# Reordering the prologue of a fused attention and feed-forward kernel: first scores ahead of the last k transposes, kv products between the second scores

## The chip, the cores and the metric

One core of one Trainium2 chip. The metric is the device time of one execution in microseconds (us), and the change is judged against the kernel before in runs on the same chip. Engine names: PE does matmuls, DVE elementwise work, ACT copies and activations, POOL is GpSimd, SP issues the transfers.

## The reference, cut to what matters

Causal linear attention with a decay per head, then a feed-forward part without an activation. B=4, H=8, S=768, D=64; d_model 512, d_ff 1536.

```python
for b in range(nb):                                   # blocks of 64 rows
    intra = einsum('bhic,bhjc->bhij', qb, kb) * Dmask
    intra = einsum('bhij,bhjd->bhid', intra, vb)
    inter = einsum('bhid,bhde->bhie', qb * lam_pow, kv_state)
    out[:, :, sl] = intra + inter
    kv_state = lam_block * kv_state + einsum('bhsd,bhse->bhde', kb_dec, vb)
x = out.transpose(0, 2, 1, 3).reshape(3072, 512)
y = ((x @ w_a) * (x @ w_b)) @ w_out
```

The kernel uses blocks of 128 rows. A **unit** is one such block of one batch with all eight heads: 24 units, six to a batch. For a unit it makes *scores* (k times q, into two PSUM banks called kq), *masks* them on DVE, forms the state st from *kv products*, and sums *intra* (mask times v) and *inter* (state times q) in a bank o; ACT copies o into xT. In profile lines m is a mask, tk, tq and tn are transposes of k, q and of k back, kvd is the eighth bank, of the third and later states, and L320 is line 320 of the kernel. Then the feed-forward part makes products a_ps and b_ps from xT and the weights, DVE multiplies them (ab), and op is the last product.

## The kernel before: the parts concerned

The units run in groups, and each unit's attention work is hung into the feed-forward slots (one a, b pair each) of the group before. Only the first group, units 0 to 3, has no feed-forward part to hide behind: its attention is the **prologue**, and PE's first a_ps waits for it.

```python
GROUPS = (4, 1, 2, 4, 4, 4, 4, 1)
PLAN = { ...                                  # slot, piece, unit; S = scores and masks
    3: [(2, "S", 11), (2, "S", 12)], ... }

def ps_bank(name, shape, dt, hold=False, ffn=False):   # seven PSUM banks, taken in turn
    i = bank["next"]
    while i in bank["held"] or (ffn and i == bank["ffn"]):
        i = (i + 1) % 7
    ...
    bank["next"] = (i + 1) % 7
    return ps_pool.tile(shape, dt, name=name, tag=f"ps{i}")

def prep_k(u):
    early = u < n0 + 3                        # n0 = 4
    make_ks(u, "dve" if early else "pool")    # k times its decay, SBUF to SBUF
    make_qs(u, "pool")
    ...
def prep_v(u):
    make_vb(u, "pool" if u < n0 + 3 else "dve")   # cast of v to bf16, SBUF to SBUF
    pump()                                        # issues further loads

# the prologue, from the transposes on
for w, parts in (("q", 1), ("k", 2)):
    for i in range(2):
        load4(w, i, parts)                    # DVE scales, PE transposes, ACT unpacks
        if w == "q":
            warm(4)                           # four matmuls without use
for u in range(n0):
    make_vb(u, "pool")
scores4(0)                                    # 16 score matmuls, 4 masks
natural_k((0, 1, 2), (0, 1))
warm(2)
natural_k((0, 1, 2), (2, 3))
warm(2)
scores4(1)                                    # the other 16, 4 masks
warm(4)
sts = [ps_bank("kv0", ...), ps_bank("kv1", ...), kv_bank()]   # the last has an eighth bank
for hh in range(2):
    for u, ps in enumerate(sts):
        for w in range(u + 1):
            kv_mms(ps, w, range(2 * hh, 2 * hh + 2), w == 0)
        if hh:
            kv_copy(u, ps, ("act", "act", "dve")[u])          # PSUM to st
intra(0); evac_o(0, *xTs[0])                  # evac_o: o to xT, on ACT if not said otherwise
intra(1); inter(1); evac_o(1, *xTs[1])
intra(2); intra(3)
inter(2); evac_o(2, *xTs[2], eng="dve")
inter(3); evac_o(3, *xTs[3])
natural_k((3,), (0, 1, 2, 3))
# ... then the feed-forward part of group 0
```

Of the kernel before, what the change touches and what calls it, by code (L numbers as in the profile page):

```python
# [17 lines left out]
BF16 = mybir.dt.bfloat16  # L18
# [4 lines left out]
def _bc(ap, dims):  # L23
# [9 lines left out]
PACK = 4  # L33
# [12 lines left out]
        (6, "S", 8), (7, "V", 7), (8, "P", 10), (9, "T", 9), (10, "V", 8), (11, "T", 10),  # L46
        (12, "Q", (7, 8, 9, 10)), (12, "P", 11), (13, "V", 9), (14, "P", 12),
        (14, "O2", (9, 10))],
    3: [(2, "S", 11), (2, "S", 12)],
}  # L50
for _g, _u in ((3, 11), (4, 15), (5, 19)):
    PLAN.setdefault(_g, []).extend(
# [9 lines left out]
def kernel(  # L62
# [11 lines left out]
    nc = tc.nc  # L74
    B, H, S, D = q.shape
    BLK = 128
    NB = S // BLK
# [27 lines left out]
    def ps_bank(name, shape, dt, hold=False, ffn=False):  # L105
# [3 lines that stand above are left out]
        if ffn:  # L109
            bank["ffn"] = i  # L110
        bank["next"] = (i + 1) % 7
        if hold:
            bank["held"].add(i)
        return ps_pool.tile(shape, dt, name=name, tag=f"ps{i}")
# [19 lines left out]
    staged = {}  # L134
# [57 lines left out]
    def warm(n, cols=128):  # L192
        for _ in range(n):
            nc.tensor.matmul(idle_ps[:, :cols], lhsT=idle_sb[:, :128], rhs=idle_sb[:, :cols],  # L194
                             start=True, stop=True, skip_group_check=True)
# [5 lines left out]
    x4 = {}  # L201
    for w, src in (("q", q), ("k", k)):
        x4_r = src[0, :, 0:PACK * BLK, :].rearrange("h (p r) d -> p h (r d)", r=PACK)
        for i in range(2):
            t = wst_pool.tile([128, 1024], F32, name=w + "4", tag="wst")
# [18 lines left out]
    ident = singles.tile([128, 128], BF16, name="ident")  # L224
# [13 lines left out]
    lp_q = singles.tile([128, NT, H, 1], F32, name="lp_q")  # L238
    lp_k = singles.tile([128, NT, H, 1], F32, name="lp_k")
# [24 lines left out]
    def make_vb(u, eng):  # L264
        vb = prep_pool.tile([128, H, D], BF16, name="vb", tag="vb")
        vf = raw.pop((u, "v"))
        if eng == "act":
            nc.scalar.copy(vb, vf)
        else:
            eng_of(eng).tensor_copy(vb, vf)  # L270
        U[u]["vb"] = vb
# [27 lines left out]
    def score_banks():  # L299
        return [ps_bank(f"kq{i}", [128, HP, 128], F32) for i in range(2)]  # L300
# [15 lines left out]
    def mask(kq):  # L316
        ms = []
        for i in range(2):
            m = msk_pool.tile([128, HP, 128], BF16, name=f"m{i}", tag=f"m{i}")
            nc.vector.tensor_mul(m, kq[i], lotri_bc)  # L320
            ms.append(m)
        return ms

    def o_bank(u):
        first = "o" not in U[u]
        if first:
            U[u]["o"] = ps_bank("o_ps", [128, HP, 128], F32)
        return first

    def inter(u):  # L330
        d = U[u]
        if u % NB > 0:
            first = o_bank(u)
            for hp in range(HP):
                nc.tensor.matmul(d["o"][:, hp, :], lhsT=st_bufs[(u - 1) % 4][:, hp, :, :],  # L335
                                 rhs=d["qT"][:, hp, :], start=(first and hp == 0), stop=True,
                                 skip_group_check=True)

    def intra(u):
        d = U[u]  # L340
        first = o_bank(u)
        for hp in range(HP):
            for i in range(2):
                p = slice(64 * i, 64 * i + 64)
                nc.tensor.matmul(d["o"][p, hp, :], lhsT=d["vb"][:, 2 * hp + i, :],  # L345
                                 rhs=d["m"](i, hp), start=(first and hp == 0),
                                 stop=True, skip_group_check=True)

    def evac_o(u, xT, col, eng="act"):
        o_ps = U[u].pop("o")  # L350
        if eng == "act":
            nc.scalar.copy(xT[:, :, col:col + BLK], o_ps)  # L352
        else:
            nc.vector.tensor_copy(xT[:, :, col:col + BLK], o_ps)

    def kv_mms(ps, w, hps, first):
        d = U[w]
        for hp in hps:
            nc.tensor.matmul(ps[:, hp, :, :], lhsT=d["kn"][:, 2 * hp:2 * hp + 2, :],  # L359
                             rhs=d["vb"][:, 2 * hp:2 * hp + 2, :], start=(first and hp == 0),  # L360
                             stop=True, skip_group_check=True)

    def kv_bank():
        kv["ps"] = kvps_pool.tile([128, HP, 2, D], F32, name="kvd", tag="kvd")
        return kv["ps"]
# [8 lines left out]
    def kv_copy(u, ps, eng="dve"):  # L374
        st = st_bufs[u % 4]
        if eng == "act":
            for i in range(2):
                p = slice(64 * i, 64 * i + 64)
                nc.scalar.copy(st[p, :, i, :], ps[p, :, i, :])  # L379
        else:  # L380
            nc.vector.tensor_mul(st[:].rearrange("p hp i d -> p hp (i d)"),  # L381
                                 ps[:].rearrange("p hp i d -> p hp (i d)"), bdiag_bc)
# [110 lines left out]
    xs4 = {"q": scr[0][:, 0:4, :], "k": scr[1][:, 0:4, :]}  # L493
    xT4 = {"q": scr[0][:, 4:8, :], "k": scr[1][:, 4:8, :]}
    kn4 = scr[1][:, 8:12, :].rearrange("p u (h d) -> p u h d", d=D)

    def load4(w, i, parts):
        dst = xs4[w].rearrange("p r (h d) -> p r h d", d=D)
        tab = lp_q if w == "q" else lp_k
        for j in range(2):  # L500
            if j == 0 or parts == 2:
                tps = ps_bank("t" + w, [128, 2, PACK, 128], BF16)
            hs = slice(4 * i + 2 * j, 4 * i + 2 * j + 2)
            nc.vector.tensor_mul(
                dst[:, :, hs, :].rearrange("p r h d -> p h r d"),
                x4[w, i][:, :, 2 * j:2 * j + 2].rearrange("p r h d -> p h r d"),
                tab[:, NB:, hs, :].rearrange("p r h o -> p h r o").to_broadcast([128, 2, PACK, D]))
            for r in range(PACK):
                nc.tensor.transpose(tps[:, j, r, :],
                                    xs4[w][:, r, hs.start * D:hs.stop * D], ident)  # L510
            if parts == 2:
                unpack(i, tps, slice(j, j + 1), w)
                if i == 0 or j == 0:
                    warm(3)
        staged.pop((w + "4", i))
        if parts == 1:
            unpack(i, tps, slice(0, 2), w)

    def unpack(i, tps, js, w):
        nc.scalar.copy(xT4[w][:, 2 * i + js.start:2 * i + js.stop, :]  # L520
                       .rearrange("c hp (p r) -> c hp p r", r=PACK),
                       tps[:, js].rearrange("c j r p -> c j p r"))

    def natural_k(us, hps):
        nu, nh = len(us), len(hps)
        tps = ps_bank("tn", [128, nu, nh, 128], BF16)
        for a, u in enumerate(us):
            for b, hp in enumerate(hps):
                nc.tensor.transpose(tps[:, a, b, :], xT4["k"][:, hp, u * BLK:(u + 1) * BLK], ident)
        nc.scalar.copy(kn4[:, us[0]:us[0] + nu, 2 * hps[0]:2 * (hps[0] + nh), :]  # L530
                       .rearrange("p u h d -> p u (h d)"),
                       tps[:].rearrange("p u j x -> p u (j x)"))

    ms4 = {}

    def scores4(i):
        kqs = []
        for up in range(PACK // 2):
            kq = score_banks()
            for uu in range(2):  # L540
                cols = slice((2 * up + uu) * BLK, (2 * up + uu + 1) * BLK)
                for j in range(2):
                    for par in range(2):
                        p = slice(64 * par, 64 * par + 64)
                        nc.tensor.matmul(kq[par][:, 2 * uu + j, :],
                                         lhsT=xT4["k"][p, 2 * i + j, cols],
                                         rhs=xT4["q"][p, 2 * i + j, cols],
                                         start=True, stop=True, skip_group_check=True)
            kqs.append(kq)
        for up, kq in enumerate(kqs):  # L550
            ms4[i, up] = mask(kq)

    for u in range(n0):
        U[u] = dict(kn=kn4[:, u], qT=xT4["q"][:, :, u * BLK:(u + 1) * BLK],
                    m=lambda i, hp, u=u: ms4[hp // 2, u // 2][i][:, 2 * (u % 2) + hp % 2, :])
    for w, parts in (("q", 1), ("k", 2)):
        for i in range(2):
            load4(w, i, parts)
            if w == "q":
                warm(4)  # L560
    for u in range(n0):
        make_vb(u, "pool")
    scores4(0)
    natural_k((0, 1, 2), (0, 1))
    warm(2)
    natural_k((0, 1, 2), (2, 3))
    warm(2)
    scores4(1)
    warm(4)
    sts = [ps_bank("kv0", [128, HP, 2, D], F32), ps_bank("kv1", [128, HP, 2, D], F32), kv_bank()]  # L570
    for hh in range(2):
        for u, ps in enumerate(sts):
            for w in range(u + 1):
                kv_mms(ps, w, range(2 * hh, 2 * hh + 2), w == 0)
            if hh:
                kv_copy(u, ps, ("act", "act", "dve")[u])
    intra(0)
    evac_o(0, *xTs[0])
    intra(1)
    inter(1)  # L580
    evac_o(1, *xTs[1])
    intra(2)
# [73 lines left out]
```

## Time and profile before

| | before |
|---|---|
| time, median of the first runs | 237.72 us (237.71 to 237.79) |
| span of the profiled execution | 235.4 us |
| busy PE, DVE, ACT, POOL | 225.1, 115.7, 92.9, 49.4 us |
| first a_ps, from the chain of waits | 19.35 us |
| PE's waits after 20 us | 0.63 at 57.46 (on DVE), 0.30 at 101.60 (on a DMA transpose) |

The lines of the prologue itself stand in the prediction.

### The profile page before, as it was taken

Reading aid. Unit: us, or ns where it says so; the run is one execution under the profiler, and the core shown is the slowest. Engines: PE = TensorE matmul, PEld = TensorE weight load, DVE = VectorE, ACT = ScalarE, POOL = GpSimd, SP = SyncE. Lnnn points to the kernel's source line nnn. Section 1 sums busy time; section 2 is a strip of 40 time slices with the busy share of each in tenths; the row PEclk is TensorE's granted clock in tenths of the full one; section 3 lists DMA queues with packets and bytes.
Section 4 is the critical chain, followed back from the end, with each engine's and each line's share of the span. In section 5 each row is a group of like instructions: output and inputs, shape, how many; then the busy total and the mean of one; then the engine's idle time right before and its main releaser. Section 6 shows DMA issues by size and latency. Waiting matters only on the chain.

```text
span 235.4 us, 4530 instructions
## 1 busy us (share of the span) xinstructions
PE 225.1 (96%) x1755; PEld 126.2 (54%) x1778; DVE 115.7 (49%) x205; ACT 92.9 (39%) x174; POOL 49.4 (21%) x63
## 2 busy tenths in 40 slices
PE   7699999998999999999999999999999999999994
PEld 2475444448698654444544454544454544444493
DVE  0886566637469637565135665135564215332050
ACT  3567654065565542341142241242341242431161
POOL 6041000245346453103306403003300000000000
PEclk9999999999999999999999999999999999999999
DMA  4999999999999999998919959523120220000311
GB/s 153 301 287 349 349 367 284 292 213 286 204 234 204 223 183 257 183 187 152 242 72 220 177 70 239 140 77 79 26 47 0 89 89 5 0 0 3 133 46 49
DMA packets 94278, 38.32 MB, mean 163 GB/s; under 512 B 81200, under 2 KB 89776, under 8 KB 94256
## 3 DMA queue, kind: packets, MB, share of 16 engines
q1 hardware_dynamic: 94112, 38.02, 71.0%
q8 instruction: 14, 0.23, 0.4%
q14 instruction: 8, 0.07, 0.1%
q10 hardware_dynamic: 144, 0.00, 0.0%
HBM read 28.32 MB, written 6.29 MB: 147 GB/s over the span
## 4 chain that ended last, share of the span: by engine, by line
PE 85%; DMA 6%; DVE 2%; ACT 2%; issue 2%; SPq 1%; DVEq 0%; ACTq 0%
PE op L434 26%; PE a_ps L413 25%; PE b_ps L413 24%; DMA k<-in_k_dram 3%; DMA qkT<-qk 3%; PE o_ps L345 2%; PE kq L308 2%; DVE m L320 2%; PE kvd L359 2%; PE o_ps L335 1%; PE tps L294 1%; ACT xT L352 1%; ACT o_sb L429 1%; SPq L206 1%; ACT st L379 1%
## 5 line engine op out<-in xcount | busy, mean ns | idle before, releaser
L425 DVE TENSOR_TENSOR ab<-a_sb,b_ps 128x512 bf16<-128x512 bf16 (+2 forms) x96 | 52.7, 553 | 82.3 <-PE b_ps L413 61.2
L413 PE MATMUL a_ps<-xT,wa_sb 128*128 128x512 bf16 (+2 forms) x378 | 76.7, 325 | 1.6 <-DVE ab L425 0.6
L413 PE MATMUL b_ps<-xT,wb_sb 128*128 128x512 bf16 (+2 forms) x379 | 76.7, 325 | 0.2
L420 ACT CAST a_sb<-a_ps 128x512 bf16<-128x512 f32 (+2 forms) x96 | 45.6, 481 | 65.6 <-PE a_ps L413 63.4
L434 PE MATMUL op<-wo_sb,ab 128*128 128x512 bf16 (+2 forms) x300 | 64.2, 362 | 0.9 <-issue 0.5
L413 PEld LDWEIGHTS <-wb_sb 128*128 128x128 bf16 x384 | 34.5, 98 | 28.7
L413 PEld LDWEIGHTS <-wa_sb 128*128 128x128 bf16 x384 | 33.5, 98 | 28.2 <-issue 1.6
L434 PEld LDWEIGHTS <-ab 128*128 128x128 bf16 x312 | 28.6, 98 | 30.2
L320 DVE TENSOR_TENSOR m<-kq,lotri 128x512 bf16<-128x512 f32 x48 | 29.9, 683 | 20.5 <-PE kq L308 19.6
L256 POOL TENSOR_TENSOR qk<-kf,lp_k 128x512 bf16<-128x512 f32 x17 | 17.9, 1053 | 76.9 <-issue 31.4
L429 ACT COPY o_sb<-op 128x512 f32<-128x512 f32 (+2 forms) x26 | 14.2, 554 | 37.2 <-PE op L434 36.7
L261 POOL TENSOR_TENSOR qk<-qf,lp_q 128x512 bf16<-128x512 f32 x20 | 23.1, 1154 | 23.8 <-DMA qf<-in_q_dram 23.8
L352 ACT CAST xT<-o_ps 128x512 bf16<-128x512 f32 x23 | 12.4, 590 | 16.9 <-PE o_ps L345 16.9
L381 DVE TENSOR_TENSOR st<-kvd,bdiag 128x512 bf16<-128x512 f32 x18 | 12.3, 684 | 3.8 <-PE kvd L359 3.8
L296 ACT COPY qkT<-tps 128x1024 bf16<-128x1024 bf16 x7 | 7.1, 1012 | 10.9 <-PE tps L294 10.9
L270 DVE CAST vb<-vf 128x512 bf16<-128x512 f32 x17 | 8.4, 496 | 0.0
L194 PE MATMUL idle<-idle_sb 128*128 128x128 bf16 (+1 forms) x38 | 7.2, 322 | 1.3 <-DVE idle_sb L189 1.3
L345 PE MATMUL o_ps<-m,vb 128*64 128x128 bf16 x192 | 7.8, 222 | 0.0
L270 POOL CAST vb<-vf 128x512 bf16<-128x512 f32 x7 | 4.3, 613 | 15.5 <-DMA vf<-in_v_dram 13.8
L308 PE MATMUL kq<-qkT 64*128 64x128 bf16 x160 | 6.7, 218 | 0.3 <-DMA qkT<-qk 0.3
L335 PEld LDWEIGHTS <-st 128*128 128x128 bf16 x80 | 5.4, 98 | 2.8
L345 PEld LDWEIGHTS <-vb 128*64 128x64 bf16 x192 | 5.7, 109 | 1.4
(52 smaller groups left out, 85.3 us busy)
## 6 DMA issues: line engine op xcount, KB each, us to landing
vf<-in_v_dram SPq DMA_DIRECT2D x24, 256.0 KB, 5.2
out_dram<-o_sb SPq DMA_DIRECT2D x23, 256.0 KB, 2.3
qf<-in_q_dram SPq DMA_DIRECT2D x20, 256.0 KB, 4.5
kf<-in_k_dram SPq DMA_DIRECT2D x20, 256.0 KB, 5.1
wst<-in_moe_w_a_dram SPq DMA_DIRECT2D x6, 512.0 KB, 8.7
wst<-in_moe_w_b_dram SPq DMA_DIRECT2D x6, 512.0 KB, 8.8
wst<-in_moe_w_out_dram SPq DMA_DIRECT2D x6, 512.0 KB, 8.5
q<-in_q_dram SPq DMA_DIRECT2D x2, 512.0 KB, 5.4
```

What stands on the lines that cost most here:

```text
L256: eng_of(eng).tensor_mul(qk[:, 1], raw.pop((u, "k")), lp_k[:, u % NB].to_broadcast([128, H, D]))
L261: eng_of(eng).tensor_mul(U[u]["qk"][:, 0], raw.pop((u, "q")), lp_q[:, u % NB].to_broadcast([128, H, D]))
L270: eng_of(eng).tensor_copy(vb, vf)
L320: nc.vector.tensor_mul(m, kq[i], lotri_bc)
L345: nc.tensor.matmul(d["o"][p, hp, :], lhsT=d["vb"][:, 2 * hp + i, :], rhs=d["m"](i, hp), start=(first and hp == 0), stop=True, skip_group_c ...
L352: nc.scalar.copy(xT[:, :, col:col + BLK], o_ps)
L381: nc.vector.tensor_mul(st[:].rearrange("p hp i d -> p hp (i d)"), ps[:].rearrange("p hp i d -> p hp (i d)"), bdiag_bc)
L413: nc.tensor.matmul(ps[:, :gt], lhsT=w_sb[:, s, f * 128:(f + 1) * 128], rhs=xT[:, s, :gt], start=(s == 0), stop=(s == KS - 1))
L420: nc.scalar.copy(a_sb[:, :gt], ps[:, :gt])
L425: nc.vector.tensor_mul(ab[:, f, :gt], a_sb[:, :gt], ps[:, :gt])
L429: nc.scalar.copy(o_sb[:, lo:hi], op[:, lo:hi])
L434: nc.tensor.matmul(op[:, lo:hi], lhsT=ab[:, f, t * 128:(t + 1) * 128], rhs=wo_sb[:, f, lo:hi], start=(f == 0), stop=(f == FC - 1))
```

## The change

The intent: the scores of the first half of the heads need no more than the first two pairs of k, so they can be issued ahead of the last k transposes, and DVE's masks start sooner. PE's wait before the second scores is then filled with kv products of units 0 and 1 in place of warm matmuls. The scores of units 11 and 12 move by one slot. The core of the diff (load4 is split into scale4 and part_k, and kv_part(u, hps) is the old inner loop over w, the kv products of one state for these head pairs; the definitions are left out):

```diff
-    3: [(2, "S", 11), (2, "S", 12)],
+    3: [(3, "S", 11), (3, "S", 12)],
...
-    for w, parts in (("q", 1), ("k", 2)):
-        for i in range(2):
-            load4(w, i, parts)
-            if w == "q":
-                warm(4)
+    ...                                # q as before
+    for i, j in ((0, 0), (0, 1), (1, 0)):
+        scale4("k", i, j)
+        part_k(i, j)
+        warm(3)
+    scale4("k", 1, 1)
     for u in range(n0):
         make_vb(u, "pool")
-    scores4(0)
+    scores4(0, (0, 1))
+    part_k(1, 1)
     natural_k((0, 1, 2), (0, 1))
     warm(2)
     natural_k((0, 1, 2), (2, 3))
     warm(2)
-    scores4(1)
-    warm(4)
     sts = [ps_bank("kv0", ...), ps_bank("kv1", ...), kv_bank()]
-    for hh in range(2): ...            # both halves of kv0, kv1, kv2, copies after the second
+    scores4(1, (0,))                   # 8 of the 16 second scores
+    kv_part(0, (0, 1))
+    kv_part(1, (0, 1))
+    scores4(1, (1,))
+    kv_part(2, (0, 1))
+    for u in range(2):
+        kv_part(u, (2, 3))
+        kv_copy(u, sts[u], "act")
     intra(0)
     evac_o(0, *xTs[0])
     intra(1)
+    kv_part(2, (2, 3))
+    kv_copy(2, sts[2], "dve")
     inter(1)
```

Because the banks are taken in turn, a change of order deals them anew. As the built order has it:

| tile | banks before | banks after | what the user waits for after the change |
|---|---|---|---|
| first scores | 6, 0, 1, 2 | 5, 6, 0, 1 | nothing that comes late |
| kv0, kv1 | 2, 3 | 5, 6 | masks 1 and 2 (before, kv0: mask 4) |
| second scores | 5, 6, 0, 1 | 0, 1, then 2, 3 | masks 3 and 4 (before: mask 1, then 2 and 3) |
| o of units 0 to 3 | 4, 5, 6, 0 | 4, 5, 6, 0 | units 1 and 2: ACT's copies of kv0 and kv1 (before: masks 5 and 6) |

More of the change, by code (lines that the diff above doesn't have):

```diff
@@ L495, with scale4, transpose4, packed_bank @@
     kn4 = scr[1][:, 8:12, :].rearrange("p u (h d) -> p u h d", d=D)
-    def load4(w, i, parts):
-        dst = xs4[w].rearrange("p r (h d) -> p r h d", d=D)
-        tab = lp_q if w == "q" else lp_k
-        for j in range(2):
-            if j == 0 or parts == 2:
-                tps = ps_bank("t" + w, [128, 2, PACK, 128], BF16)
-            hs = slice(4 * i + 2 * j, 4 * i + 2 * j + 2)
-            nc.vector.tensor_mul(
-                dst[:, :, hs, :].rearrange("p r h d -> p h r d"),
-                x4[w, i][:, :, 2 * j:2 * j + 2].rearrange("p r h d -> p h r d"),
-                tab[:, NB:, hs, :].rearrange("p r h o -> p h r o").to_broadcast([128, 2, PACK, D]))
-            for r in range(PACK):
-                nc.tensor.transpose(tps[:, j, r, :],
-                                    xs4[w][:, r, hs.start * D:hs.stop * D], ident)
-            if parts == 2:
-                unpack(i, tps, slice(j, j + 1), w)
-                if i == 0 or j == 0:
-                    warm(3)
-        staged.pop((w + "4", i))
-        if parts == 1:
-            unpack(i, tps, slice(0, 2), w)
+    def scale4(w, i, j):
+        hs = slice(4 * i + 2 * j, 4 * i + 2 * j + 2)
+        nc.vector.tensor_mul(
+            xs4[w].rearrange("p r (h d) -> p h r d", d=D)[:, hs],
+            x4[w, i][:, :, 2 * j:2 * j + 2].rearrange("p r h d -> p h r d"),
+            (lp_q if w == "q" else lp_k)[:, NB:, hs, :].rearrange("p r h o -> p h r o")
+            .to_broadcast([128, 2, PACK, D]))
+        if j == 1:
+            staged.pop((w + "4", i))
+    def transpose4(w, i, j, tps):
+        h = 4 * i + 2 * j
+        for r in range(PACK):
+            nc.tensor.transpose(tps[:, j, r, :], xs4[w][:, r, h * D:(h + 2) * D], ident)
+    def packed_bank(w):
+        return ps_bank("t" + w, [128, 2, PACK, 128], BF16)
+    def part_k(i, j):
+        tps = packed_bank("k")
+        transpose4("k", i, j, tps)
+        unpack(i, tps, slice(j, j + 1), "k")
     def unpack(i, tps, js, w):
@@ L534, with scores4 @@
     ms4 = {}
-    def scores4(i):
+    def scores4(i, ups):
         kqs = []
-        for up in range(PACK // 2):
+        for up in ups:
             kq = score_banks()
@@ L549, in scores4 @@
             kqs.append(kq)
-        for up, kq in enumerate(kqs):
+        for up, kq in zip(ups, kqs):
             ms4[i, up] = mask(kq)
@@ L555 @@
                     m=lambda i, hp, u=u: ms4[hp // 2, u // 2][i][:, 2 * (u % 2) + hp % 2, :])
-    for w, parts in (("q", 1), ("k", 2)):
-        for i in range(2):
-            load4(w, i, parts)
-            if w == "q":
-                warm(4)
+    for i in range(2):
+        tps = packed_bank("q")
+        for j in range(2):
+            scale4("q", i, j)
+            transpose4("q", i, j, tps)
+        unpack(i, tps, slice(0, 2), "q")
+        warm(4)
+    for i, j in ((0, 0), (0, 1), (1, 0)):
[3 more added lines that the diff above has]
+    scale4("k", 1, 1)
     for u in range(n0):
         make_vb(u, "pool")
-    scores4(0)
+    scores4(0, (0, 1))
+    part_k(1, 1)
     natural_k((0, 1, 2), (0, 1))
@@ L567, with kv_part @@
     warm(2)
-    scores4(1)
-    warm(4)
     sts = [ps_bank("kv0", [128, HP, 2, D], F32), ps_bank("kv1", [128, HP, 2, D], F32), kv_bank()]
-    for hh in range(2):
-        for u, ps in enumerate(sts):
-            for w in range(u + 1):
-                kv_mms(ps, w, range(2 * hh, 2 * hh + 2), w == 0)
-            if hh:
-                kv_copy(u, ps, ("act", "act", "dve")[u])
+    def kv_part(u, hps):
+        for w in range(u + 1):
+            kv_mms(sts[u], w, hps, w == 0)
+    scores4(1, (0,))
[6 more added lines that the diff above has]
+        kv_copy(u, sts[u], "act")
     intra(0)
```

## The prediction

> **What bounds the kernel now.** I read the page first. PE is busy in 225.1 of 235.4 us and the chain that ended last is PE for 85%: almost all of it is the feed-forward products (a_ps, b_ps, op). In the row of 40 slices PE stands at 9 from the second or third slice to the last but one, and the granted clock at 9 (full) everywhere. So a change outside the feed-forward part can only pay through the moment at which its first matmul starts, and through the few waits of PE afterwards. Next I read the chain of waits from 0 to 24 us, because that is where this change acts; these are its lines from the last k transposes to that first matmul (start, duration, what):
>
> ```profile
> 11.69 0.40 PE tk L509 x4
> 12.09 0.38 PE kq L545 x8
> 12.46 0.01 DVEq L320
> 12.47 0.04 issue
> 12.52 1.90 DVE m L320 x3
> 14.42 0.04 issue
> 14.46 0.38 PE kq L545 x7
> 14.84 0.33 PE idle L194 x4
> 15.17 0.48 PE kv L359 x6
> ...
> 17.34 0.37 ACT st L379
> 17.71 0.02 issue
> 17.73 1.57 ACT xT L352 x3
> 19.30 0.04 issue
> 19.35 0.38 PE a_ps L413
> ```
>
> The reader is to see three hand-overs: masks on DVE free a bank for the second scores; kv products feed the four st copies on ACT; ACT then makes three xT copies back to back, and the last releases the first a_ps at **19.35**. The timelines of DVE, ACT and PE from 5 to 24 us show how full those stretches are:
>
> ```profile
> 12.52 4.88 DVE L320 TENSOR_TENSOR m<-kq,lotri 128x512 bf16<-128x512 f32 x8 [0.89 <-PE kq L545]
> 17.31 0.68 DVE L381 TENSOR_TENSOR st<-kvd,bdiag 128x512 bf16<-128x512 f32 x1
> ...
> 16.19 1.52 ACT L379 CAST st<-kv 64x256 bf16<-64x256 f32 x4 [1.57 <-PE kv L359]
> 17.73 1.56 ACT L352 CAST xT<-o_ps 128x512 bf16<-128x512 f32 x3
> ```
>
> DVE runs eight masks without a gap, one every 0.60 us; ACT is without a gap from 16.19 to 19.29. Beyond that, PE's waits after 20 us are 0.63 at 57.46 (on DVE), 0.30 at 101.60 (unit 14's DMA transpose) and crumbs.
>
> **What the Trainium skill says.** "TensorE: Matmul & The Clock Gate", section "The mechanism", says that matmuls start and end strictly in program order. So a matmul that waits for its bank holds back everything behind it; the trace agrees, the warm matmuls and kv products stand still behind the scores that wait 0.39 us for a mask at 14.46. The same page, "What's actually happening", puts the fall of the clock at about 3.4 us of idleness; the longest idle time here is under 1.3 us and the clock stays full, and I count on that below. "PSUM — Partial Sum Buffer", section "PSUM bank collisions raise a hardware error", asks that PSUM be guarded by bank rather than by address; the kernel does so, each tile has a bank of seven taken in turn, and its next user waits for the last reader. That decides this case.
>
> **The change part by part.** I followed the turns of the banks and the waits in the built instruction order.
>
> *First scores earlier.* In the old order they start at 12.02, behind the last k transposes, which wait for DVE until 11.69. Now they follow the third k transposes (11.08, four at 0.056 = 0.23) and three warm matmuls (0.17), plus the 0.1 us that the old trace takes between transposes and scores: 11.59, a gain of **0.43**. DVE's last scaling ends at 11.63, so it does not hold the masks: they start at 12.09, the fourth starts at 13.89 and ends at 14.58 (0.68 long).
>
> *Second scores later.* Before, their banks were those of the last k transposes, then of masks 1, 2 and 3, so nine of sixteen ran at 13.57 and the rest at 14.46. Now the two banks of the kv products are taken first (from masks 1 and 2), and the very first scores need the banks of masks 3 and 4. So eight scores start at 14.62. The seven behind the wait take 0.31 as before: 14.93. Mask 5 starts at 15.17 instead of 14.92, DVE has a gap of about 0.5, and mask 8 ends at 17.65 instead of 17.40. The gain of 0.43 is spent.
>
> *kv in between, four warm matmuls gone.* From 14.93: six kv products (6 x 0.056 = 0.33), eight scores (0.31), six kvd products (0.33), the two that finish kv0 (0.11), and 0.2 for three changes of kind: issue ends at 16.21, the last start is one slot of 0.056 earlier, a product lasts 0.22, so kv0 is complete at 16.37 and the first st copy starts at **16.4**, against 16.19. Before, kv0 itself waited for mask 4 (its semaphore at 15.0), with 14 products and no scores behind the wait.
>
> *New waits.* The outputs o of units 1 and 2 now get the banks of kv0 and kv1, so intra(1) waits until ACT has copied st0 and intra(2) until it has copied st1. Before they had the banks of masks 5 and 6 and did not wait: PE ran intra 0 and 1 at 16.58 as one block of 16. Now intra(0) runs at 16.45, ACT's two st0 copies take 0.75 and end at 17.16, and intra(1) starts at 17.2. Behind it, in order: eight intra 0.28, a change 0.06, six kvd 0.33, inter(1) 0.22, a change 0.1, sixteen intra 0.57, eight inter 0.45, two changes 0.15 = 2.16, so the last inter(3) issues by 19.3 and lands near 19.5. st2 is on the same road (kvd ends 18.07, DVE to 18.8) but does not come last. ACT has done xT of units 0 and 1 by 19.0, so the last xT waits for PE: 19.5 + 0.59 = 20.1, first a_ps at **20.15**. That is **+0.8**.
>
> *Scores of units 11 and 12 one slot later.* One slot is an a, b pair, 1.73 us. At the old place they start at 91.38 without a wait, and the masks follow DVE's product at once; one slot on it is the same picture, with four masks (2.48) before the next product and the same rotation of banks. Their masks are used ten microseconds later, at 101.9. I count **0**; it gives the transpose of unit 12 slack that the old trace does not need.
>
> **How much of 0.8 arrives.** PE is full afterwards, so a late start moves the end one for one, except where PE waits for a transfer that does not move with it. The wait at 101.60 can swallow up to 0.3: DMA share is 9 tenths until about 112 us and its queue there is issued without gaps. The wait at 57.46 follows DVE work tied to PE's own slots and stays. So +0.5 to +0.8. I shade it down a little, to **+0.5**, because a turn of banks that I misread would remove the largest term: 237.72 + 0.5 = 238.2.
>
> **Rivals.** *The reorder pays as meant:* the masks start 0.43 earlier, the kv products fill PE's wait, and everything moves up, 237.3. For it: DVE's eight masks are a gapless 4.88 us that end at 17.40, and starting them earlier is the right aim. Against it: mask 5 cannot start before scores that now wait for mask 4. It needs ACT's st copies to start by 15.9. *Absorbed altogether:* if the DMA sets the pace to 112 us, a late start is caught up at the waits for loads and transposes, 237.7. For it: DMA at 9 tenths for half the run. Against: PE shows only 0.30 of wait on DMA after 20 us, and a wait can't give back more than it has. *A wait at the moved scores:* if masks one slot later hold DVE's products and PE finds no free bank, up to 0.6 more, 238.8. For it: the like stall at 57.46, after scores. Against: no stall followed the same block at slot 2.
>
> **Range and chances.** The three cases and the main one lie between 237.3 and 238.9, all within 0.5%. Repeats spread 0.08 us. A change of 2% is 4.75 us, more than the whole idle time that could be won (10.3 us of PE idle, half of it before the first q arrives) and six times the loss that I find. Range 237.4 to 238.8; faster 0.01, same 0.98, slower 0.01.
>
> **What would show each step.** Right: first scores at 11.6 and masks from 12.1; a PE wait on a mask until about 14.6; a gap inside DVE's masks; PE waiting on ACT's st copies at intra(1), near 17.2; first a_ps near 20.1; the wait for unit 14's transpose gone or smaller. Wrong: a_ps before 19.35 would mean that ACT got kv0 much earlier than 16.4, so that I have the banks or the issue rates wrong. A first a_ps near 20.1 with an unchanged total would mean the absorption; a clock below full early on, or new idle time of PE near 94, would mean causes that I left out.

## More of the kernel before

How to read it: each digit of this cut from the page of the kernel before is the busy share of one of 40 slices, in tenths.

```profile
PE   7699999998999999999999999999999999999994
DVE  0886566637469637565135665135564215332050
POOL 6041000245346453103306403003300000000000
DMA  4999999999999999998919959523120220000311
```

The 8 of PE's row is the slice from 53.0 to 58.9 us; POOL and DVE both work there, and that turns out to matter.

## The result, and the profile after

The changed kernel took **238.24 us** (median of four runs: 238.01, 237.62, 238.69, 238.46) against 237.72 of the kernel before (four runs, 237.71 to 237.79). The ratio is 1.0019 [0.9995, 1.0044], so the two are the same within 2%. Ratios here and below are the mean time of one kernel's fast runs over that of the other's of the same rounds, so not quite the ratio of the medians quoted; a ratio is turned into us by 237.5. All outputs are right.

The prologue of the changed kernel, from its chain of waits (start, duration, what):

```profile
12.12 2.50 DVE m L320 x4
...
14.66 0.38 PE kq L546 x7
15.04 0.44 PE kv L359 x6
15.48 0.33 PE kq L546 x8
15.81 0.44 PE kvd L359 x6
16.25 0.13 PE kv L359 x2
...
16.46 0.18 ACT st L379
...
17.26 0.41 PE o_ps L345 x8
...
19.49 0.59 ACT xT L352
20.09 0.04 issue
20.13 1.89 PE a_ps L413 x8
```

The masks start at 12.12 instead of 12.52, and yet the second scores start at 14.66 instead of 14.46: they now wait for the fourth mask. Scores and three groups of kv products follow without a gap, so ACT gets kv0 at 16.46 instead of 16.19. The first a_ps is at 20.13 instead of 19.35, **0.78 later**.

The timeline of DVE in the changed kernel (start, duration, count at the end, in brackets the idle time before it and what ended it):

```profile
12.12 2.49 DVE L320 TENSOR_TENSOR m<-kq,lotri 128x512 bf16<-128x512 f32 x4 [0.46 <-PE kq L546]
15.04 2.48 DVE L320 TENSOR_TENSOR m<-kq,lotri 128x512 bf16<-128x512 f32 x4 [0.43 <-PE kq L546]
```

The eight masks that ran as one block of 4.88 us are now two blocks with 0.43 us of idle time between them. What the early start gained, this gap spends: DVE releases the last masks at 17.52 instead of 17.40.

Now the rest of the run. PE's shift (time after less time before, same instructions) is +0.78 at the first a_ps, +0.42 at 57.46, +0.71 at 74.82, +0.22 at 101.93, and a constant +0.39 from 116 us to PE's last instruction. (The +0.22 is of one moment: the next a_ps, at 102.50 before, is already 0.40 late.) So half of the lateness seen at 20 us was gone in the end, and not in a straight line. Two places matter. The first, from the timelines of all engines, kernel before:

```profile
55.62 1.04 POOL L256 TENSOR_TENSOR qk<-kf,lp_k 128x512 bf16<-128x512 f32 x1 [1.40 <-DMA kf<-in_k_dram]
56.17 1.04 DVE L256 TENSOR_TENSOR qk<-kf,lp_k 128x512 bf16<-128x512 f32 x1
56.62 1.49 POOL L261 TENSOR_TENSOR qk<-qf,lp_q 128x512 bf16<-128x512 f32 x1
...
57.46 0.38 PE L413 MATMUL a_ps<-xT,wa_sb 128*128 128x128 bf16 x4 [0.63 <-DVE ab L425]
```

and the same of the changed kernel:

```profile
56.03 1.04 POOL L256 TENSOR_TENSOR qk<-kf,lp_k 128x512 bf16<-128x512 f32 x1 [2.26 <-DMA kf<-in_k_dram]
56.95 0.68 DVE L256 TENSOR_TENSOR qk<-kf,lp_k 128x512 bf16<-128x512 f32 x1
57.03 1.50 POOL L261 TENSOR_TENSOR qk<-qf,lp_q 128x512 bf16<-128x512 f32 x1
...
57.88 0.33 PE L413 MATMUL a_ps<-xT,wa_sb 128*128 128x128 bf16 x3 [0.27 <-DVE ab L425]
```

The DVE line is the k scaling of unit 6, with both inputs in SBUF. It took 1.04 us before and 0.68 after, and PE's wait behind it fell from 0.63 to 0.27, exactly as much. So 0.36 of the old wait is time that DVE stood still; the other 0.27 is there too when the scaling is not held, and no wait is left where the scaling is taken off DVE (below). In the kernel before, the scaling starts while POOL's k scaling of the next unit runs, and it ends at 57.21, 0.59 after POOL's hand-over at 56.62; POOL's next instruction then lasts 1.49 instead of 1.04. In the changed kernel DVE arrives at 56.95, just as POOL finishes, and gets in ahead of POOL's next one. The Trainium skill has this: "SBUF — State Buffer", section "Who interferes with whom", says that DVE and GpSimd share one pair of ports as an exclusive lock, held for a whole instruction while the loser stands still, and that a DVE instruction with two SBUF inputs contends with a GpSimd instruction that reads SBUF. The traces agree: in each of these meetings one of the two instructions is long.

The second place is the wait on unit 14's DMA transpose, from the timelines of PE, before and after:

```profile
101.60 0.40 PE L308 MATMUL kq<-qkT 64*128 64x128 bf16 x8 [0.30 <-DMA qkT<-qk]
```

```profile
101.60 0.62 PE L308 MATMUL kq<-qkT 64*128 64x128 bf16 x16
```

The 0.30 us of waiting is gone: the eight scores of the unit run in one block with the eight of the unit ahead, and PE's shift falls from 0.70 at 100.58 to 0.40 at 102.50.

Working the other way, DVE's casts of v, which also copy from SBUF to SBUF, became longer. From the page, before and after (busy us, mean ns):

```profile
L270 DVE CAST vb<-vf 128x512 bf16<-128x512 f32 x17 | 8.4, 496 | 0.0
```

```profile
L270 DVE CAST vb<-vf 128x512 bf16<-128x512 f32 x17 | 9.5, 559 | 0.0
```

A cast takes 0.42 undisturbed and up to 1.18 us in these two profiles when it meets POOL. One of them, at 71.86 in the changed kernel, took 0.90 instead of 0.42 (at 71.43) and stands ahead of the masks on DVE; that is where the shift of PE went up again to +0.71.

The profiled span grew by 0.9 where PE's end moved by 0.39. The other 0.5 lies in the last stores, which ended later after PE in that one execution; the next profile of the same kernel had the tail of the kernel before.

### The profile page after: what moved, and what is told of

It reads as the page before. It is cut to its first block, busy times and chain, and to the rows that moved or that the text cites. A ratio compares the mean times of both kernels' runs of the same rounds, so it can differ in the third digit from the quotient of the medians.

```text
span 236.3 us, 4544 instructions
## 1 busy us (share of the span) xinstructions
PE 227.3 (96%) x1774; PEld 126.3 (53%) x1774; DVE 116.6 (49%) x205; ACT 92.8 (39%) x174; POOL 49.1 (21%) x63
## 4 chain that ended last, share of the span: by engine, by line
PE 90%; DMA 3%; DVE 2%; ACT 2%; issue 1%; SPq 1%; DVEq 0%; ACTq 0%
PE a_ps L413 27%; PE b_ps L413 26%; PE op L434 26%; DMA k<-in_k_dram 3%; PE o_ps L345 2%; PE kq L308 2%; PE kvd L359 2%; PE o_ps L335 2%; PE tps L294 1%; DVE m L320 1%; ACT o_sb L429 1%; SPq L206 1%; ACT xT L352 0%; PE kq L546 0%; DVE scratch L499 0%
## 5 line engine op out<-in xcount | busy, mean ns | idle before, releaser
L434 PE MATMUL op<-wo_sb,ab 128*128 128x512 bf16 (+2 forms) x312 | 65.6, 363 | 0.0
L352 ACT CAST xT<-o_ps 128x512 bf16<-128x512 f32 x23 | 12.5, 590 | 16.9 <-PE o_ps L345 16.4
L270 DVE CAST vb<-vf 128x512 bf16<-128x512 f32 x17 | 9.5, 559 | 0.0
```

The source lines that it names most:

```text
L270: eng_of(eng).tensor_copy(vb, vf)
L352: nc.scalar.copy(xT[:, :, col:col + BLK], o_ps)
L434: nc.tensor.matmul(op[:, lo:hi], lhsT=ab[:, f, t * 128:(t + 1) * 128], rhs=wo_sb[:, f, lo:hi], start=(f == 0), stop=(f == FC - 1))
```

## The experiments

Theory after the first look: **the late start is real and explains the whole loss; behind it the DVE and POOL lock and one DMA wait give part of it back or add to it, according to how the two engines happen to meet.** Rivals: (R1) the slot move costs or gains something; (R2) the loss is not the start but something else that the new prologue brings, say transfers; (R3) the scatter of the changed kernel is noise of the chip and has nothing to do with the lock. Five rounds were run of each kernel, on three chips, with runs of the kernel before in each; first a_ps is from the one profiled execution of each.

### The changed kernel again

No edit.

> The changed kernel once more, for its interval. Theory (a late start of the feed-forward part, 0.78 us at the first a_ps, partly given back at later waits): 0.3 to 0.8 us over the kernel before, first a_ps at 20.1. Rival (the 0.5 us between the two medians is only the scatter of the end of the run): within 0.15 us of the kernel before.

238.27 us (237.81 to 239.18, six runs) against 237.28 of the kernel before; ratio 1.0048 [1.0029, 1.0067], some 1.1 us. First a_ps at 20.11. So it is slower by an interval that excludes zero, though still the same by the bound of 2%, and by more than the 0.3 to 0.8 us that were expected. Its runs scatter by 1.4 us: over both sets the ten runs lie from 237.62 to 239.18. The scaling of unit 6 took 0.78 this time. The kernel before in these rounds: 236.44 to 237.80 over eleven runs, so its own spread is not the 0.08 us of the first three runs either.

### The prologue alone

In the changed kernel:

```diff
-    3: [(3, "S", 11), (3, "S", 12)],
+    3: [(2, "S", 11), (2, "S", 12)],
```

> The new prologue with the scores of units 11 and 12 at their old slot 2. Theory (the slot costs nothing, all comes from the prologue): first a_ps at 20.1 and a total within 0.3 us of the changed kernel. Rival (the later slot itself costs or pays): a total at least 0.4 us away from the changed kernel, and new PE idle time near 91 us or near 102 us.

237.91 us (237.51 to 239.22), ratio 1.0036 [1.0016, 1.0057], not to be told apart from the changed kernel. First a_ps at 20.07. Its profiled execution was the slowest of the six, and its timeline shows why a run can be slow:

```profile
55.87 1.04 POOL L256 TENSOR_TENSOR qk<-kf,lp_k 128x512 bf16<-128x512 f32 x1 [2.08 <-DMA kf<-in_k_dram]
56.87 1.04 POOL L261 TENSOR_TENSOR qk<-qf,lp_q 128x512 bf16<-128x512 f32 x1
56.89 1.56 DVE L256 TENSOR_TENSOR qk<-kf,lp_k 128x512 bf16<-128x512 f32 x1
```

DVE came at 56.89, when POOL's second instruction had started at 56.87. It stood still until POOL was done and ended at 58.45, and PE waited 1.15 us behind it. In the changed kernel DVE came at 56.95 and POOL's second instruction at 57.03, with DVE first. A few hundredths of a us decide between a wait of 0.27 and one of 1.15.

### The slot move alone

In the kernel before:

```diff
-    3: [(2, "S", 11), (2, "S", 12)],
+    3: [(3, "S", 11), (3, "S", 12)],
```

> The kernel before, with only the scores of units 11 and 12 one slot later. Theory (the slot is worth nothing): first a_ps at 19.35 as before, scores at 93.1, total within 0.25 us of the kernel before. Rival (the slot carries part of the 0.5 to 1 us): a total 0.4 us or more above the kernel before, with a longer PE wait near 101.6.

237.67 us (237.47 to 237.84) against 237.48; ratio 1.0009 [0.9997, 1.0020]. First a_ps at 19.30. The move costs at most half a us and probably nothing. In its profile the scaling of unit 6 came early enough to be ahead of POOL (0.68), so PE was ahead by 0.4 at 57 (and the moved scores started at 92.70, not 93.1); then it waited 1.15 us at 102.04 for unit 14's transpose, 0.85 more than the kernel before. That longer wait is the sign that the rival named, but the trace does not lead it back to the moved scores: POOL's k scaling after a load was late before they ran (88.03 against 87.52 in the kernel before), the transpose was issued at 95.75 instead of 95.32, and PE came 0.4 earlier. So R1 is out for the size of the loss; one profile can't exclude a small share.

### The start delayed in the kernel before

```diff
     scores4(1)
-    warm(4)
+    warm(18)
```

> The kernel before with 14 more warm matmuls ahead of the kv products, 14 x 0.056 = 0.78 us of pure delay and no other change of order or bank. Theory (only the late start counts): kv products at 15.9, first a_ps at 20.1, PE waits near 57 and 101 smaller than before, and a total 0.3 to 0.6 us over the kernel before, like the changed kernel. Rival (the new order costs by itself later on): first a_ps at 20.1, yet a total within 0.2 us of the kernel before.

238.20 us (237.62 to 238.47), ratio 1.0038 [1.0022, 1.0054]; first a_ps at 20.09. The old prologue with nothing but a start as late as in the changed kernel costs as much as the changed kernel does. So R2 is not needed: the late start is enough. The loss, 0.9 us, is more than the 0.3 to 0.6 expected, and one of the expected signs failed: the wait near 57 grew. The scaling of unit 6 started at 56.91 behind a POOL instruction that had begun at 56.59, and took 1.26; PE waited 0.85 there and nothing at 102.

### The two kv banks withheld from o

In the changed kernel, so that o of units 1 and 2 get other banks and do not wait for ACT's copies:

```diff
     scores4(1, (1,))
     kv_part(2, (0, 1))
+    bank["held"].update((5, 6))
```

> The changed kernel, but the outputs o of units 1 and 2 may not take the banks of kv0 and kv1. Theory (intra(1) waits for the two st0 copies because of the shared bank, and that is on the path): the wait before intra(1) goes, intra(1) at 16.8, st2 on DVE near 17.7, first a_ps at 19.65, that is 0.45 to 0.5 earlier than 20.13 and 0.3 later than before; total 0.1 to 0.4 us over the kernel before. Rival (only the late st copies on ACT set the start): first a_ps stays near 20.1.

First a_ps at 19.61, half a us earlier, and the 16 intra matmuls are one block again. The timeline of ACT in this kernel:

```profile
16.46 1.51 ACT L379 CAST st<-kv 64x256 bf16<-64x256 f32 x4 [1.86 <-PE kv L359]
18.00 1.56 ACT L352 CAST xT<-o_ps 128x512 bf16<-128x512 f32 x3
```

The st copies start when they did in the changed kernel, and now the three xT copies follow without a gap, where the changed kernel's last one waited for PE. So of the 0.78, some 0.5 is the new wait for the kv banks, and the remaining 0.27 is the later st copy. The time was 237.82 (237.66 to 238.12), ratio 1.0025 [1.0012, 1.0038]: of the half us some 0.3 to 0.5 arrived (1.0025 against 1.0036 and 1.0048, with intervals that overlap), and the distance to the kernel before, 0.6, is above the 0.1 to 0.4 expected. The scaling of unit 6 took 1.23 in the profile, and PE waited 0.82.

### A prologue that does what was meant

In the changed kernel the banks are dealt by hand and the kv products of units 0 and 1 go entirely ahead of the last eight scores, with the st copies:

```diff
+    bank["next"] = 5
+    scores4(1, (0,))
+    bank["next"] = 2
     sts = [ps_bank("kv0", ...), ps_bank("kv1", ...), kv_bank()]
...
-    scores4(1, (0,))
     kv_part(0, (0, 1))
     kv_part(1, (0, 1))
-    scores4(1, (1,))
-    kv_part(2, (0, 1))
     for u in range(2):
         kv_part(u, (2, 3))
         kv_copy(u, sts[u], "act")
+    bank["next"] = 0
+    scores4(1, (1,))
+    bank["next"] = 4
+    kv_part(2, (0, 1))
     intra(0)
```

> The changed kernel with the banks dealt anew: the first four second scores take the banks of masks 1 and 2, kv0 and kv1 those of early k transposes, and kv0 and kv1 are finished before the rest of the second scores. Theory: no wait for mask 4 ahead of kv, first st copy on ACT near 15.0, masks on DVE without a gap and ended at 17.0, first a_ps at 18.7 to 18.8, 0.6 before the kernel before; total 0.1 to 0.8 us below it, by how the scalings near 57 fall. Rival (the start is bound by DVE or by the k load, whatever the banks): first a_ps at 19.3 or later.

The timelines of DVE and ACT in this kernel:

```profile
12.11 4.87 DVE L320 TENSOR_TENSOR m<-kq,lotri 128x512 bf16<-128x512 f32 x8 [0.45 <-PE kq L546]
```

```profile
15.03 1.51 ACT L379 CAST st<-kv 64x256 bf16<-64x256 f32 x4 [0.44 <-PE kv L359]
...
18.31 0.59 ACT L352 CAST xT<-o_ps 128x512 bf16<-128x512 f32 x1 [0.53 <-PE o_ps L335]
```

The masks are one block again and start early, the st copies begin at 15.03, and the first a_ps is at 18.95: 1.2 us ahead of the changed kernel and 0.4 ahead of the kernel before (0.6 was expected). So the aim of the change was sound: masks that start early can bring the first a_ps forward. This variant changes the banks and also the order, so it does not show that the banks alone defeated the change; what they cost through o is the 0.5 of the run before. The time, 236.86 (235.97 to 237.74), ratio 0.9976 [0.9957, 0.9996], scatters by 1.8 us.

### The same kernels with the meetings of DVE and POOL removed

Two edits take the two kinds of SBUF to SBUF instruction that met POOL off DVE: the k scaling of unit 6 goes to POOL, the casts of v from unit 7 on go to ACT. They were applied to the kernel before, the changed kernel, and the two variants above:

```diff
-        early = u < n0 + 3
+        early = u < n0 + 2
...
-        make_vb(u, "pool" if u < n0 + 3 else "dve")
+        make_vb(u, "pool" if u < n0 + 3 else "act")
```

> The kernel before, with the k scaling of unit 6 moved from DVE to POOL and the v casts of units 7 and later moved from DVE to ACT, so that no DVE instruction of the stretch from 55 to 80 us can be held up by a POOL instruction. Theory (the PE wait at 57.46 and the later ones come from DVE operations held until POOL's current one ends): the wait of 0.63 near 57 goes, total 0.5 to 0.9 us below the kernel before. Rival (DMA sets the pace there): the wait moves to a load, total unchanged.

> The changed kernel with the same two moves. Theory: first a_ps at 20.1, no wait near 57, so the late start of 0.78 us arrives nearly whole: 0.5 to 0.8 us above before_nolock, and single runs within 0.5 us of each other where the changed kernel spreads over 1.3 us. Rival (the scatter and the give-back come from DMA): spread as wide as that of the changed kernel, difference to before_nolock under 0.4 us.

> after_nolock, with the banks of kv0 and kv1 kept from the outputs o. Theory (the shared bank costs 0.5 us of the 0.78 at the start, and without the scalings and casts on DVE it arrives): first a_ps at 19.6 to 19.7, total 0.3 to 0.55 us below after_nolock, within 0.35 us of before_nolock. Rival (the bank wait was hidden by something else in the end): total within 0.15 us of after_nolock.

> early_st (first a_ps at 18.95) with the same two moves off DVE. Theory: no wait near 57, spread under 0.5 us where early_st spread over 1.8, total 0.3 to 0.7 us below before_nolock, so 235.6 to 236.0. Rival (DMA, that is the transpose of unit 14 near 101, caps what an early start can win): a PE wait there of 0.5 us or more and a total within 0.2 us of before_nolock.

| kernel, without the meetings | first a_ps | time, us | ratio to before | in us |
|---|---|---|---|---|
| early st | 18.99 | 235.62 (235.51 to 235.72) | 0.9923 [0.9911, 0.9934] | -1.8 |
| before | 19.64 | 236.27 (236.01 to 236.42) | 0.9949 [0.9937, 0.9961] | -1.2 |
| changed, kv banks withheld | 19.66 | 236.38 (236.04 to 236.52) | 0.9950 [0.9937, 0.9963] | -1.2 |
| changed | 20.20 | 236.81 (236.74 to 236.97) | 0.9974 [0.9962, 0.9986] | -0.6 |

The time follows the first a_ps one for one: 1.21 us from the first row to the last in both columns (20.20 less 18.99; 0.0051 times 237.5). The spread from the lowest to the highest run fell from 1.4 to 0.2 us in the changed kernel, from 1.8 to 0.2 in the early st variant, from 0.7 to 0.4 in the kernel before (same rounds), and stayed at 0.5 in the one with withheld banks. (The 1.4 and the 0.2 of the changed kernel are of two chips; on the chip of the 0.2, the early st variant spread by its 1.8 and the kernel before by 0.7.) One caution: the 19.64 of the kernel before is of an execution whose first q load came late (19.30 and 19.35 in two others with the same prologue), and that kernel kept a wait of 0.24 us on unit 14's transpose. A start of about 19.35 plus that wait gives the same place.

R3 falls: the large scatter goes when these instructions leave DVE. The kernel before gained 1.2 us, more than the 0.5 to 0.9 expected. The edits also take the scaling and 17 casts off DVE altogether, so how much of the 1.2 us is the lock and how much is a DVE with less to do is not separated by these runs; at the wait near 57 of the kernel before it was 0.36 and 0.27.

The early st variant with these edits beats both kernels, by 1.85 us against 237.47 of the kernel before in its rounds.

### Only the k scaling of unit 6 moved

```diff
-        early = u < n0 + 3
+        early = u < n0 + 2
```

in the changed kernel, casts left on DVE.

> The changed kernel with only the k scaling of unit 6 moved to POOL; the v casts stay on DVE. Theory (the scaling that meets POOL's pair near 57 us makes most of the scatter, the v casts near 72 and 76 the rest): no PE wait near 57, spread about half that of the changed kernel, total about 237.2 to 237.8. Rival (the v casts make it all): spread over 1 us still, total near 238.2.

237.48 us (237.08 to 237.84), ratio 1.0001 [0.9987, 1.0014]; first a_ps at 20.12, and no wait near 57. The standard deviation of its runs is 0.32 us, against 0.54 of the changed kernel's six and 0.09 with the casts moved too. So this one instruction on DVE is part of the scatter and of the loss: without it the late start no longer shows in the time against the kernel before, which still has it. How the casts share the rest with the lighter load of DVE stays open, as said.

### One thing seen, not settled

Unit 14's transpose took 6.1 to 6.3 us from issue to landing in all four kernels with the old prologue, and 4.6 to 5.0 in all nine with a new one. The DMA's busy tenths from 98 to 101 us and the queue of instruction fetches in that stretch, kernel before:

```profile
DMA  9999999999999000000001000010000079999999
q8 instruction: 1, 0.02, 2.6%
```

and the DMA's row of the changed kernel, where no fetch falls into the stretch:

```profile
DMA  9999999999999999999900079999998689999999
```

In the four old ones one fetch of 0.02 MB falls between 98 and 99 us, within the transpose, and for over a us the queues move nearly nothing; in the nine others that fetch comes at 101 us or later. This is thirteen profiles agreeing, and no experiment: why the fetch moved, and whether it holds up the transpose, is open.

## Why the prediction was right, and where its steps were not

- **First scores and masks.** Predicted 11.59 and 12.09, found 11.62 and 12.12. Right.
- **Second scores wait for mask 4.** Predicted 14.62, found 14.66, with one score ahead of it at 14.06. The gap inside the masks was to be 0.5 and was 0.43. Right.
- **First st copy** 16.4, found 16.46; **intra(1) waits for ACT** at 17.2, found 17.26 with 0.33 us of waiting; **last xT waits for PE** at 19.5, found 19.49; **first a_ps** 20.15, found 20.13. Right, and the withheld banks show the term of the kv banks alone: 0.5 of the 0.78.
- **Slot move, 0.** The run of it alone gives 1.0009 with an interval that holds 1. Right.
- **The wait at 101.60 can swallow up to 0.3.** It did vanish. In the delayed kernel before, with the old transposes, it vanished for the reason given: PE came later. In the changed kernel there was a second reason, a transpose that landed sooner (5.0 us after its issue instead of 6.2), which the prediction had not seen. Nor did the transfer stay where it was, as the prediction had assumed: it was issued at 95.89 instead of 95.32.
- **"The wait at 57.46 follows DVE work tied to PE's own slots and stays."** This step failed. The wait was 0.27 to 0.37 in the two profiles of the changed kernel and 1.15 in the one with the prologue alone. What varies in it is DVE held by POOL, and POOL's pair starts, in most of the profiles, when a load lands (55.6 to 56.4 in those with the scaling on DVE), not when PE gets there. A later PE meets POOL in another phase.
- **"Repeats spread 0.08 us."** Failed too: the changed kernel spreads by 1.6 us over ten runs and the kernel before by up to 1.4, so three close runs said little about the spread.
- **"10.3 us of PE idle, half of it before the first q arrives."** A wrong reading without effect on the rest: PE's idle time before its first q transposes (6.58) is 2.1 us; 2.2 more lie before the first a_ps, and 3.3 after the last matmul.
- **The shading to +0.5** was given for a doubt about the banks, and the banks were as read, so that it met the first runs (0.5) is luck; the next ones gave 1.1. The sum without the shading gives the same: 0.8 of late start less 0.3 of waiting that it swallows is 0.5, and with the meetings removed the changed kernel is 0.54 us behind the kernel before (236.81 against 236.27).
- **The rivals.** "Pays as meant" needed st copies by 15.9; they came at 16.46, and the variant in which they came at 15.03 did pay. "Absorbed altogether" fell with the delayed start, which cost 0.9 us. "A wait at the moved scores": none showed.

So the measured 238.24 against 238.2 is right mostly by its main term, and closer than the argument deserved: the next set of runs of the same kernel gave 1.0048 instead of 1.0019.

## What to carry to other kernels

When buffers are taken in turn, an exchange of two steps deals all later ones anew: write down, for each new owner, whose last reader it now waits for, before counting what the exchange gains. If one kernel's repeats scatter more than another's, look for an instruction whose duration takes several values, and for two engines that meet at a moment set by different things (here PE's slots and a load's landing). And an instruction off the critical engine that stands still for a lock looks busy, so compare its duration with that of the same shape elsewhere before believing it.

## What the Trainium skill lacked or had wrong

- "SBUF — State Buffer", section "Who interferes with whom", has the exclusive lock, and the runs agree. It lacks how the lock looks in a profile: the DVE instruction that is held counts as busy (0.68 us grows to 1.04, 1.26 and 1.56 for the same shape), with no idle time before it and no waiter named, and PE's wait behind it is put down to a later DVE instruction. POOL's held instruction likewise shows 1.49 instead of 1.04.
- "TensorE: Matmul & The Clock Gate", section "Back-to-back issue gap", gives about 81 ns (N=128) and 131 ns (N=512) as the sustained spacing of matmuls in a stream, and says that the formula for an isolated one under- and over-counts. Here the isolated figures fit the streams instead: in the changed kernel eight inter products (N=128) take from 18.84 to the next start at 19.29, 0.056 us each, and eight a_ps matmuls (N=512) from 20.13 to the next start at 21.85, 0.215 us each.
- "Runtime: NRT & Kernel Launch", section "Instruction fetch mechanics", says that a fetch has its own queue and is mostly hidden. It says nothing of a fetch beside a DMA transpose; the transpose took 6.1 to 6.3 us in the profiles with a fetch inside it and 4.6 to 5.0 in those where the fetch came later (seen together, not tested).
